# Block bounds by VectorE and one small product, in an attention and soft-MoE kernel

## The chip, the cores and the metric

The kernel runs on one core of one Trainium2 chip. The metric is the device time of one execution in microseconds (us). The times given for a kernel are those of repeated executions; one further execution was taken with the hardware profiler, and all rows of the trace come from that one.

Names used below: TensorE (PE in the profile; PEld its weight loads) does the matrix products and writes them into PSUM, 16 KB for each of 128 partitions in eight banks of 512 float32 values; VectorE (DVE) and ScalarE (ACT) read and write both PSUM and the on-chip SBUF; SyncE (SP) issues the DMAs.

## The reference, cut to what matters

```python
def _attn_ref(u, v, z):                  # u, v: (8, 2496, 256)   z: (8, 2496, 64)
    scores = (1.0 / S) * np.matmul(z, z.transpose(0, 2, 1))
    attn = np.maximum(scores, 0.0) ** 2
    return u * np.matmul(attn, v)

def _moe_ref(x, phi, w1, w2):            # x: (19968, 256)   phi: (256, 32)
    logits = x @ phi
    d = softmax of logits over all tokens (axis 0);  c = softmax over the 32 slots (axis 1)
    slot_input = (d.T @ x).reshape(8, 4, 256)
    slot_out[e] = np.maximum(slot_input[e] @ w1[e], 0.0) @ w2[e]    # for each of 8 experts
    return c @ slot_out.reshape(32, 256)
```

The inputs u, v and z are normal numbers times 0.1. Nothing of their size is assumed by the kernel: it scales blocks of z and v by powers of two before it splits them into a high and a low float16 part.

## The kernel before, in words

**Tiles.** A batch has 2496 rows, stored as five key blocks of 512 (the last padded). z of a block is a tile of 128 partitions by 512: the 64 features stand on the partitions, twice over. v of a block is two tiles of 128 by 512. Queries are worked through in chunks of 512 (chunk 4 of a batch is padded and has 448 columns). A chunk meets the five blocks in ten **halves** (256 keys each), so a batch has 50 halves, and the loop at the end of the kernel takes one half h per turn, called a step here. "Step 39" without a batch means the 40th step of a batch, the last half of chunk 3.

**A step.** `sums_halves` or `sums_whole` multiplies the half's attention (a high part ph and a low part pl) with v into the chunk's accumulator, a PSUM tile `acc` of two banks; the pool `acc_ps` holds two of them. In the same step `prepare` makes a half that comes two or three steps later: scores on TensorE (`sc`), Relu and Square on ScalarE (`r`), a cast to ph on ScalarE or VectorE, and pl by VectorE. Since z z^T is symmetric, half of the attention is transposed by VectorE (`y`), stored to DRAM (`turned`) and loaded again instead of being computed. When a chunk ends, `finish_chunk` multiplies its accumulator by u and by a factor (`out_by`) into `xg`. From `xg` the soft-MoE part is worked off in small pieces, one per step from the list `work`: logits, exponentials, transposes, sums of slots (`lg` in the trace).

**Order.** All engines keep the program order (class `InOrder`). Work that is to follow a prepared half is put on the list `behind`, which `prepare` runs at its end. `landing[h]` holds what joins `behind` in step h.

**Bounds and factors.** For each block of z in a batch b >= 1, `load_z` issues the load; two steps later `measure` lets ScalarE square the block (`squares`, tile sq), and again two or more steps later TensorE adds the squares over the features with a matrix of ones (`norms`, tile n in the trace, a PSUM tile of tag "ms") and VectorE takes the largest over each half block into `tops`. When five blocks are done, `factors` turns the largest sums into powers of two: `norm2` and, as its inverse root, `z_by`. v is handled by `load_v` (squares with a row sum into `energy`), `largest` in step 38 and `scale_v` in step 41: the latter spreads v's largest value over the partitions with two small products (mx in the trace, also of tag "ms"), VectorE reduces them into `few`, and `v_by` and `out_by` follow. The tag "ms" has one buffer (line 92), shared by n, mx and lg. `measure` keeps n and lg at least two steps apart.

**Opening.** For the first batch the same is written out ahead of the loop: squares and norms of the five blocks go to the tiles `n_first`, `n_second` and `idle`; the first halves are scored from raw float32 z (`zraw`, tile cw) scaled in place by `raise_z`; `keep_busy` issues matmuls whose result isn't used.

Of the kernel before, what the change touches and what calls it, by code (L numbers as in the profile page):

```python
# [8 lines left out]
F32 = mybir.dt.float32  # L9
# [9 lines left out]
P = 128  # L19
# [6 lines left out]
QC = 512  # L26
# [35 lines left out]
def bits(ap):  # L62
    return ap.bitcast(I32)
# [14 lines left out]
def attn_soft_moe_kernel(ctx, tc, uT, v, zz, phi, ww, outT):  # L78
# [29 lines left out]
    def pair(name, n):  # L108
# [3 lines left out]
        pair(name, n)  # L112
        for name, n in (("tops", 2 * NP), ("norm2", NP), ("z_by", NP), ("energy", 2 * NP), ("v_by", 2 * NP), ("out_by", NP), ("few", 4))
    )
# [9 lines left out]
    def load_z(b, j):  # L124


        if b == 0:
            raw = cw[:, 19 + 4 * j : 23 + 4 * j].rearrange("p g n -> p (g n)")
        else:
            raw = raws.tile([P, 512], F32, tag="raw", name=f"zr_{b}_{j}", bufs=NRAW)  # L130
        sp.dma_start(raw, zz[b, :, j * 512 : (j + 1) * 512])
        zraw[b, j] = raw
        by = z_by[b % 2][:, j : j + 1]
        square = []

        def squares():
            sq = raws.tile([P, 512], BF16, tag="sq", name=f"sq_{b}_{j}", bufs=2)
            act.activation(sq, raw, AF.Square, bias=nudge)
            square.append(sq)

        def norms(ps=None):
            if ps is None:
                ps = ms_ps.tile([P, 2, 512], F32, tag="ms", name=f"n2_{b}_{j}")[:, :, 0:256]
            for h, rows in enumerate(HALF):
                pe.matmul(
                    ps[:, h], ones[rows, 0:P], square[0][rows, 256 * h : 256 * h + 256],
                    start=True, stop=True,
                )
            dve.tensor_reduce(tops[b % 2][:, 2 * j : 2 * j + 2], ps, axis=AX.X, op=ALU.max)

        def split():
            t = zt[b, j]
            if b == 0:
                act.copy(t[:, 0], raw)
                dve.tensor_sub(t[:, 1], raw, t[:, 0])
            else:
                act.activation(t[:, 0], raw, AF.Identity, scale=by)
                dve.scalar_tensor_tensor(
                    t[:, 1], raw, by, t[:, 0], op0=ALU.mult, op1=ALU.subtract
                )  # L160

        return squares, norms, split
# [44 lines left out]

    def scale_v(b):


        w = few[b % 2]
        ps = ms_ps.tile([P, 2, 512], F32, tag="ms", name=f"mx_{b}")
        for h, rows in enumerate(HALF):
            pe.matmul(
                ps[:, h, 0:64], w[rows, 0:1].to_broadcast([64, P]), ident[rows, rows],
                start=True, stop=True,
            )
        dve.tensor_reduce(w[:, 2:4], ps[:, :, 0:64], axis=AX.X, op=ALU.max)
        dve.scalar_tensor_tensor(w[:, 1:2], w[:, 2:3], 2.0**-120, w[:, 3:4], op0=ALU.max, op1=ALU.max)
# [13 lines left out]
    def open_loads():  # L233
        for p in range(NP):
            *two, z_splits[p] = load_z(0, p)
            first_z.append(two)
        order = [i for p in range(NP) for i in ((2 * p + 1, 2 * p) if p == NQ - 1 else (2 * p, 2 * p + 1))]
# [344 lines left out]

    late, adding, bursts = [], [], []

# [20 lines left out]
    def groups(q):  # L605
# [17 lines left out]
        def logits():  # L623
# [4 lines left out]
            for c in range(2):  # L628
                for t in range(4):
                    for h, rows in enumerate(HALF):  # L630
# [3 lines left out]
                        )  # L634
            bursts.append(q)
            if late:
# [225 lines left out]
    for b in range(1, B):  # L862
# [12 lines left out]
    unmeasured, squared, used = [], [], [-9, 0]  # L875

    def measure(h, scoring):


        n = h % (2 * NP * NQ)  # L880
        if squared and squared[0][0] <= h - 2 and used[0] <= h - 2 and (scoring or n >= 26):
            behind.append(squared.pop(0)[1])
            used[0] = h
            used[1] += 1
            if used[1] % NP == 0:
                behind.append(lambda: factors(used[1] // NP))
        if unmeasured and unmeasured[0][0] <= h and len(squared) < 2:
            _, squares, norms = unmeasured.pop(0)
            behind.append(squares)
            squared.append((h, norms))  # L890

    def transfers(h):
# [14 lines left out]
        for f, b, i, at in splits.get(h + 2, ()):  # L907
            if (b, 0) not in vt_:
                take_blocks(b)
            if f is load_z:  # L910
                *two, split = f(b, i)
                unmeasured.append((h + 2, *two))
                landing.setdefault(at, []).append(split)
                continue
            for step, g in zip(at, f(b, i), strict=True):
# [38 lines left out]
    keep_busy(6)  # L954
    places = [ms_ps.tile([P, 2, 512], F32, tag="ms", name="n2_first")]
    places.append(acc_ps.tile([P, 2, QC], F32, tag="acc", name="n2_second"))
    places = [t[:, :, 256 * i : 256 * i + 256] for t in places for i in range(2)] + [idle[:, :, 0:256]]

    def raise_z(p):
# [5 lines left out]

    for p in range(NP):
        first_z[p][0]()
    first_z[0][1](places[0])
    factors(0, slice(0, 1))
    raise_z(0)  # L970
    for p in range(1, NP):
        keep_busy(1)
        first_z[p][1](places[p])
    factors(0, slice(1, NP))
    raise_z(1)
    for p in range(4):
        measure_v((2, 2, 1, 1)[p])
        prepare(p)
        if p < 3:
            raise_z(p + 2)  # L980
    keep_busy(8)
    measure_v(4)
    largest(0)
    scale_v(0)
    split_first_v()
    acc = None
    for h, x in enumerate(halves):
        if x.begins:
            acc = acc_ps.tile([P, 2, QC], F32, tag="acc", name=f"acc_{x.ch[3]}")
        last = len(halves) - h  # L990
        transfers(h)
        weights(last)
        if work and (x.at > 1 or last <= 20):
            n = len(bursts)
            work.pop(0)()
            if len(bursts) > n:
                used[0] = h
# [328 lines left out]
```

## Time and profile before

| | us |
|---|---|
| median of 3 runs | 1378.52 (1377.18 to 1385.05) |
| profiled execution | 1376.17 |
| its span, first to last instruction | 1374.0 |
| mean granted TensorE clock | 0.977 |

How to read it: the span lies 2.2 us under the time of the same execution, and that time 2.35 us under the median. A page of the profile gives busy time of each engine; the view of the waits lists how long an engine stood idle and whose end released it; the timeline lists instructions in order of time with their start, their length and, in brackets, the idle time before them and its releaser. In the trace all instructions have one line number (L74, the helper that keeps the order), so they are told apart by the names of their tiles, written "out<-in".

### The profile page before, as it was taken

Reading aid. Unit: us, or ns where it says so; the run is one execution under the profiler, and the core shown is the slowest. Engines: PE = TensorE matmul, PEld = TensorE weight load, DVE = VectorE, ACT = ScalarE, POOL = GpSimd, SP = SyncE. Lnnn points to the kernel's source line nnn. Section 1 sums busy time; section 2 is a strip of 40 time slices with the busy share of each in tenths; the row PEclk is TensorE's granted clock in tenths of the full one; section 3 lists DMA queues with packets and bytes.
Section 4 is the critical chain, followed back from the end, with each engine's and each line's share of the span. In section 5 each row is a group of like instructions: output and inputs, shape, how many; then the busy total and the mean of one; then the engine's idle time right before and its main releaser. Section 6 shows DMA issues by size and latency. Waiting matters only on the chain.

```text
span 1374.0 us, 27763 instructions
## 1 busy us (share of the span) xinstructions
PE 1275.1 (93%) x11029; PEld 618.3 (45%) x11029; DVE 1102.6 (80%) x1553; ACT 960.5 (70%) x1260; POOL 3.7 (0%) x22
## 2 busy tenths in 40 slices
PE   6998999899999999899999999989999999989984
PEld 2343445344544444344544444444454444434852
DVE  5687789688997799777998799877897799867663
ACT  6776778476876678567886678667786678754453
POOL 0000000000000000000000000000000000000000
PEclk9999999999999999999999999999999999999995
DMA  4566827777486856868287766868376776979959
GB/s 141 145 207 188 265 86 205 244 231 240 102 252 213 266 161 168 278 223 273 73 224 242 258 191 159 268 215 257 94 216 227 257 240 172 264 224 295 339 214 384
DMA packets 136401, 298.87 MB, mean 218 GB/s; under 512 B 17872, under 2 KB 38864, under 8 KB 124240
## 3 DMA queue, kind: packets, MB, share of 16 engines
q1 hardware_dynamic: 136272, 297.11, 69.4%
q8 instruction: 86, 1.41, 0.4%
q14 instruction: 43, 0.35, 0.1%
HBM read 162.04 MB, written 113.77 MB: 201 GB/s over the span
## 4 chain that ended last, share of the span: by engine, by line
PE 46%; ACT 17%; DVE 13%; DMA 11%; SPq 7%; issue 5%; DVEq 0%; ACTq 0%; POOLq 0%
PE acc L74 35%; ACT r L74 9%; SPq L74 7%; PE sc L74 5%; DMA turned<-y 5%; ACT ph L74 4%; DVE pl L74 4%; DVE y L74 4%; PE lg L74 2%; DMA vr<-in_v 2%; PE pf L74 1%; ACT vq L74 1%; DMA w_own<-in_w 1%; DVE ph L74 1%; DMA zr<-in_zz 1%
## 5 line engine op out<-in xcount | busy, mean ns | idle before, releaser
L74 PE MATMUL acc<-ph,v 64*128 64x512 f16 (+5 forms) x5036 | 934.9, 370 | 4.2 <-ACT v L74 1.8
L74 PEld LDWEIGHTS <-v 64*128 64x128 f16 (+1 forms) x7554 | 475.4, 95 | 525.8 <-issue 44.0
L74 PE MATMUL acc<-pl,v 64*128 64x512 f16 (+5 forms) x2518 | 604.1, 369 | 2.7 <-DVE pl L74 2.1
L74 DVE TENSOR_TENSOR pl<-r,ph 128x1024 f16<-128x1024 f32 (+1 forms) x410 | 466.5, 1146 | 146.6 <-ACT ph L74 133.7
L74 ACT CAST ph<-r 128x1024 f16<-128x1024 f32 (+1 forms) x286 | 287.5, 1017 | 87.6 <-DMA r<-turned 49.9
L74 ACT ACTIVATE r<-sc 128x1024 f32<-128x1024 f32 (+1 forms) x242 | 229.0, 946 | 140.6 <-PE sc L74 138.7
L74 ACT ACTIVATE r<-r 128x1024 f32<-128x1024 f32 (+1 forms) x242 | 238.5, 986 | 6.9
L74 DVE STREAM_TRANSPOSE y<-r 128x1024 f32<-128x1024 f32 x160 | 197.9, 1237 | 0.0
L74 PE MATMUL sc<-z,z 64*128 64x512 f16 x912 | 124.7, 377 | 7.8 <-ACT r L74 7.5
L74 PEld LDWEIGHTS <-z 64*128 64x128 f16 x1380 | 71.8, 94 | 86.0 <-issue 19.2
L74 DVE CAST ph<-r 128x1024 f16<-128x1024 f32 (+1 forms) x124 | 73.9, 596 | 21.9 <-ACT r L74 21.5
L74 ACT ACTIVATE vq<-vr 128x512 bf16<-128x512 f32 x80 | 49.8, 623 | 50.3 <-DMA vr<-in_v 49.8
L74 ACT ACTIVATE v<-vr,v_by 128x512 f16<-128x512 f32 x80 | 56.9, 715 | 11.8 <-DVE v_by L74 11.8
L74 DVE SCALAR_TENSOR_TENSOR xg<-acc,out_by,ut 128x1024 f32<-128x1024 f32 (+7 forms) x57 | 51.8, 931 | 13.3 <-PE acc L74 13.2
L74 DVE SCALAR_TENSOR_TENSOR v<-vr,v_by,v 128x512 f16<-128x512 f32 x80 | 57.8, 724 | 0.7 <-ACT v L74 0.7
L74 PE MATMUL sc<-z 64*128 64x512 f16 (+1 forms) x468 | 50.9, 321 | 2.9 <-ACT r L74 2.9
L74 PE MATMUL lg<-xg,phi_sb 64*32 64x256 f32 x608 | 25.5, 443 | 29.0 <-DVE tops L74 16.9
L74 DVE STREAM_TRANSPOSE y<-xg 128x512 f32<-128x512 f32 x72 | 49.4, 686 | 0.0
L74 ACT ACTIVATE sq<-zr,nudge 128x512 bf16<-128x512 f32 x35 | 25.0, 714 | 24.8 <-DMA zr<-in_zz 24.8
L74 DVE COPY ot<-pf 128x1024 f32<-128x1024 f32 (+1 forms) x20 | 24.0, 1198 | 20.6 <-PE pf L74 16.5
L74 ACT COPY ot<-pf 128x1024 f32<-128x1024 f32 (+1 forms) x20 | 19.8, 991 | 24.3 <-PE pf L74 18.1
L74 DVE TENSOR_TENSOR pl<-rd,ph 128x512 f16<-128x512 f32 x36 | 24.0, 668 | 11.3 <-ACT ph L74 11.1
(184 smaller groups left out, 579.7 us busy)
## 6 DMA issues: line engine op xcount, KB each, us to landing
turned<-y SPq DMA_DIRECT2D x320, 256.0 KB, 4.8
r<-turned SPq DMA_DIRECT2D x76, 1024.0 KB, 6.0
xt<-y SPq DMA_DIRECT2D x288, 72.0 KB, 2.9
vr<-in_v SPq DMA_DIRECT2D x80, 256.0 KB, 5.6
outT<-ot SPq DMA_DIRECT2D x18, 1024.0 KB, 7.4
ut<-in_uT SPq DMA_DIRECT2D x31, 512.0 KB, 5.6
lent<-yd SPq DMA_DIRECT2D x144, 64.0 KB, 2.8
rd<-lent SPq DMA_DIRECT2D x36, 256.0 KB, 4.0
```

Source lines behind the costliest of these rows:

```text
L74: return lambda *a, **k: self.tc.keep_in_program_order(f(*a, **k))
```

## The change

The bound of a z block is now the sum over the features of the largest square of each feature. VectorE takes the largest square of each of the 128 partitions in one instruction (`bound`), in place of ScalarE's squares, the product with ones and VectorE's reduction. When the five blocks are done, one product with a 128x128 matrix of ones adds the 128 values of each block (`add_bounds`), and `factors` reads the result. `add_bounds` runs in step 25 of a batch, `factors` in step 26; the product is written into the accumulator of the next chunk (chunk 3), which `next_acc` allocates for it ahead of time. `largest` moves from step 38 to 37 and `scale_v` from 41 to 39; its two products go into columns 448 to 511 of chunk 4's accumulator. `measure` and its guards are gone. In the opening the five bounds stand in VectorE's program order with their factors, all products go to `idle`, all of v's squares are taken after half 1 is prepared, and halves 2 and 3 are prepared after `scale_v`, half 2 ahead of the first split of v and half 3 behind it.

```diff
-        (("tops", 2 * NP), ("norm2", NP), ... , ("few", 4))
+        (("tops", NP), ("norm2", NP), ... , ("few", 4))
...
-        def squares():
-            sq = raws.tile([P, 512], BF16, tag="sq", name=f"sq_{b}_{j}", bufs=2)
-            act.activation(sq, raw, AF.Square, bias=nudge)
-            square.append(sq)
-
-        def norms(ps=None):
-            if ps is None:
-                ps = ms_ps.tile([P, 2, 512], F32, tag="ms", name=f"n2_{b}_{j}")[:, :, 0:256]
-            for h, rows in enumerate(HALF):
-                pe.matmul(
-                    ps[:, h], ones[rows, 0:P], square[0][rows, 256 * h : 256 * h + 256],
-                    start=True, stop=True,
-                )
-            dve.tensor_reduce(tops[b % 2][:, 2 * j : 2 * j + 2], ps, axis=AX.X, op=ALU.max)
+        def bound():
+            sq = raws.tile([P, 512], BF16, tag="sq", name=f"sq_{b}_{j}", bufs=1)
+            dve.tensor_tensor_reduce(
+                sq, raw, raw, 1.0, 2.0**-80, op0=ALU.mult, op1=ALU.max,
+                accum_out=tops[b % 2][:, j : j + 1],
+            )
...
-    def factors(b, js=slice(0, NP)):
+    def add_bounds(b, ps, js):
+        pe.matmul(
+            ps[:, 0, js], nc.const_aps.tensor(1.0, [P, P], F32), tops[b % 2][:, js], start=True, stop=True
+        )
+
+    def factors(b, ps, js):
...
-        t = tops[b % 2].rearrange("p (j h) -> p h j", h=2)[:, :, js]
-        dve.tensor_max(n2, t[:, 0], t[:, 1])
-        dve.tensor_scalar(bits(n2), bits(n2), EVEN, None, op0=ALU.bitwise_and)
+        dve.tensor_scalar(bits(n2), bits(ps[:, 0, js]), EVEN, None, op0=ALU.bitwise_and)
...
-    def scale_v(b):
+    def scale_v(b, ps):
...
-        ps = ms_ps.tile([P, 2, 512], F32, tag="ms", name=f"mx_{b}")
+        ps = ps[:, :, 2 * PAD :]
         for h, rows in enumerate(HALF):
             pe.matmul(
-                ps[:, h, 0:64], w[rows, 0:1].to_broadcast([64, P]), ident[rows, rows],
+                ps[:, h], w[rows, 0:1].to_broadcast([64, P]), ident[rows, rows],
                 start=True, stop=True,
             )
-        dve.tensor_reduce(w[:, 2:4], ps[:, :, 0:64], axis=AX.X, op=ALU.max)
+        dve.tensor_reduce(w[:, 2:4], ps, axis=AX.X, op=ALU.max)
...
         for i, (j, at) in enumerate(zip(order, z_at)):
-            splits.setdefault(base + 11 + 2 * i, []).append((load_z, b, j, base + at))
+            splits.setdefault(base + 11 + 2 * i, []).append((load_z, b, j, [base + 14 + 2 * i, base + at]))
...
-        later[base + 38] = lambda b=b: largest(b)
-        later[base + 41] = lambda b=b: scale_v(b)
+        later[base + 37] = lambda b=b: largest(b)
+        later[base + 39] = lambda b=b: scale_v(b, next_acc())
+        later[base + 25] = lambda b=b: add_bounds(b, next_acc(), slice(0, NP))
+        later[base + 26] = lambda b=b: factors(b, accs[-1], slice(0, NP))
...
-    def measure(h, scoring):
...
+    def next_acc():
+
+        accs.append(acc_ps.tile([P, 2, QC], F32, tag="acc", name=f"acc_{len(accs)}"))
+        return accs[-1]
...
-    for p in range(NP):
-        first_z[p][0]()
-    first_z[0][1](places[0])
-    factors(0, slice(0, 1))
-    raise_z(0)
-    for p in range(1, NP):
-        keep_busy(1)
-        first_z[p][1](places[p])
-    factors(0, slice(1, NP))
-    raise_z(1)
-    for p in range(4):
-        measure_v((2, 2, 1, 1)[p])
-        prepare(p)
-        if p < 3:
-            raise_z(p + 2)
+    for js in (slice(0, 1), slice(1, 2), slice(2, NP)):
+        for p in range(*js.indices(NP)):
+            first_z[p]()
+        add_bounds(0, idle, js)
+        factors(0, idle, js)
+        if js.start < 2:
+            raise_z(js.start)
+            keep_busy(2)
+    prepare(0)
+    measure_v(2)
+    prepare(1)
+    measure_v(8)
     keep_busy(8)
-    measure_v(4)
+    for p in range(2, NP):
+        raise_z(p)
     largest(0)
-    scale_v(0)
+    scale_v(0, idle)
+    prepare(2)
     split_first_v()
+    prepare(3)
     acc = None
     for h, x in enumerate(halves):
         if x.begins:
-            acc = acc_ps.tile([P, 2, QC], F32, tag="acc", name=f"acc_{x.ch[3]}")
+            chunk = h // (2 * NP)
+            acc = accs[chunk] if chunk < len(accs) else next_acc()
...
-        measure(h, ahead and not halves[ahead[0]].turned)
```

More of the change, by code (lines that the diff above doesn't have):

```diff
@@ L112, in attn_soft_moe_kernel @@
         pair(name, n)
-        for name, n in (("tops", 2 * NP), ("norm2", NP), ("z_by", NP), ("energy", 2 * NP), ("v_by", 2 * NP), ("out_by", NP), ("few", 4))
+        for name, n in (("tops", NP), ("norm2", NP), ("z_by", NP), ("energy", 2 * NP), ("v_by", 2 * NP), ("out_by", NP), ("few", 4))
     )
@@ L133, in load_z @@
         by = z_by[b % 2][:, j : j + 1]
-        square = []
-        def squares():
-            sq = raws.tile([P, 512], BF16, tag="sq", name=f"sq_{b}_{j}", bufs=2)
-            act.activation(sq, raw, AF.Square, bias=nudge)
-            square.append(sq)
-        def norms(ps=None):
-            if ps is None:
-                ps = ms_ps.tile([P, 2, 512], F32, tag="ms", name=f"n2_{b}_{j}")[:, :, 0:256]
-            for h, rows in enumerate(HALF):
-                pe.matmul(
-                    ps[:, h], ones[rows, 0:P], square[0][rows, 256 * h : 256 * h + 256],
-                    start=True, stop=True,
-                )
-            dve.tensor_reduce(tops[b % 2][:, 2 * j : 2 * j + 2], ps, axis=AX.X, op=ALU.max)
+        def bound():
[4 more added lines that the diff above has]
+            )
         def split():
@@ L160, in split @@
                 )
-        return squares, norms, split
-    def factors(b, js=slice(0, NP)):
+        return bound, split
+    def add_bounds(b, ps, js):
[3 more added lines that the diff above has]
+    def factors(b, ps, js):
         n2, by = (t[b % 2][:, js] for t in (norm2, z_by))
-        t = tops[b % 2].rearrange("p (j h) -> p h j", h=2)[:, :, js]
-        dve.tensor_max(n2, t[:, 0], t[:, 1])
-        dve.tensor_scalar(bits(n2), bits(n2), EVEN, None, op0=ALU.bitwise_and)
+        dve.tensor_scalar(bits(n2), bits(ps[:, 0, js]), EVEN, None, op0=ALU.bitwise_and)
         dve.tensor_scalar(
@@ L234, in open_loads @@
         for p in range(NP):
-            *two, z_splits[p] = load_z(0, p)
-            first_z.append(two)
+            bound, z_splits[p] = load_z(0, p)
+            first_z.append(bound)
         order = [i for p in range(NP) for i in ((2 * p + 1, 2 * p) if p == NQ - 1 else (2 * p, 2 * p + 1))]
@@ L581, in finish_chunk @@
             s += w
-    late, adding, bursts = [], [], []
+    late, adding = [], []
     xt_last = []
@@ L634, in logits @@
                         )
-            bursts.append(q)
             if late:
@@ L871, in attn_soft_moe_kernel @@
             )
-        later[base + 38] = lambda b=b: largest(b)
-        later[base + 41] = lambda b=b: scale_v(b)
+        later[base + 37] = lambda b=b: largest(b)
+        later[base + 39] = lambda b=b: scale_v(b, next_acc())
+        later[base + 25] = lambda b=b: add_bounds(b, next_acc(), slice(0, NP))
+        later[base + 26] = lambda b=b: factors(b, accs[-1], slice(0, NP))
     landing, fetched = {}, set()
-    unmeasured, squared, used = [], [], [-9, 0]
-    def measure(h, scoring):
[L880 to L890, printed above, removed]
+    accs = []
+    def next_acc():
+        accs.append(acc_ps.tile([P, 2, QC], F32, tag="acc", name=f"acc_{len(accs)}"))
+        return accs[-1]
     def transfers(h):
@@ L909, in transfers @@
                 take_blocks(b)
[L910 to L914, printed above, removed]
             for step, g in zip(at, f(b, i), strict=True):
@@ L954, in attn_soft_moe_kernel @@
     keep_busy(6)
-    places = [ms_ps.tile([P, 2, 512], F32, tag="ms", name="n2_first")]
-    places.append(acc_ps.tile([P, 2, QC], F32, tag="acc", name="n2_second"))
-    places = [t[:, :, 256 * i : 256 * i + 256] for t in places for i in range(2)] + [idle[:, :, 0:256]]
     def raise_z(p):
@@ L993, in attn_soft_moe_kernel @@
         if work and (x.at > 1 or last <= 20):
-            n = len(bursts)
             work.pop(0)()
-            if len(bursts) > n:
-                used[0] = h
         behind.extend(landing.pop(h, ()))
         ahead = [k for k in range(h + 2 + (h > CATCH), h + 3 + (h >= CATCH)) if k < len(halves) and k >= 4]
-        measure(h, ahead and not halves[ahead[0]].turned)
         split_first_v()
```

## The prediction

> **What bounds the kernel now.** I read the page first, then the waits of TensorE, then the timeline around each of those waits, and only then the other engines.
>
> ```profile
> span 1374.0 us, 27763 instructions
> PE 1275.1 (93%) x11029; PEld 618.3 (45%) x11029; DVE 1102.6 (80%) x1553; ACT 960.5 (70%) x1260; POOL 3.7 (0%) x22
> ```
>
> TensorE is busy for 93% of the span, so the question is what its 99 us of idle time consist of. The view of the waits, for TensorE alone, answers it:
>
> ```profile
> PE lg L74 <- DVE tops L74: 16.9, 4, 4.7
> ...
> PE lg L74 <- DVE few L74: 12.1, 4, 3.3
> PE n L74 <- DVE tops L74: 8.8, 9, 1.8
> ...
> PE mx L74 <- DVE few L74: 3.6, 2, 3.2
> PE n L74 <- DVE slot_acc L74: 3.0, 3, 1.0
> ```
>
> The first column is the total, then the number of waits, then the longest. All five rows have one cause: the tag "ms" has a single buffer, and logits (lg), norms (n) and the product for v's factor (mx) take turns in it. TensorE may not write the next until VectorE, which runs some us behind, has read the last. 3.2 us of the mx row are in the opening, so 16.9 + 12.1 + 8.8 + 3.0 + 0.4 = **41.2 us** of idle TensorE in the steady part hang on the buffer that this change leaves to the logits alone.
>
> Some of these waits cost more than their length:
>
> ```profile
> 268.75 1.96 PE L74 MATMUL lg<-xg,phi_sb 64*32 64x256 f32 x32 [4.72 <-DVE tops L74]
> 270.46 1.90 PE L74 MATMUL lg<-xt 64*32 64x256 f32 x32
> ...
> 517.41 1.09 PE L74 MATMUL lg<-xg,phi_sb 64*32 64x256 f32 x32
> 518.30 1.07 PE L74 MATMUL lg<-xt 64*32 64x256 f32 x32
> ...
> 268.70:270.00 1.30, 1.25 (x24) 0.67 (x32) 0.00 (x0) 0.00 (x0) 0.00 (x0) 0.52 0.43 105
> ...
> 173.32 1.96 PE L74 MATMUL lg<-xg,phi_sb 64*32 64x256 f32 x32 [3.30 <-DVE few L74]
> ...
> 962.86 1.10 PE L74 MATMUL lg<-xg,phi_sb 64*32 64x256 f32 x32 [3.17 <-DVE few L74]
> ```
>
> The same burst of 64 matmuls takes 3.61 us after a wait of 4.72 us (268.75 to 272.36) and 1.96 us without one (517.41 to 519.37). The row of the windows view shows why: the granted clock (third number from the end) is 0.52. A wait of 3.30 us still has it (1.96 for 32 matmuls), one of 3.17 us has not (1.10). So a wait over about 3.2 us costs 1.65 us on top. Five of the eight logits waits are that long (the four for tops and the first for few); I count 1.5 each, 7.6 us.
>
> **The change, part by part.** *What goes.* The 41.2 us of waits and 7.6 us of half clock. Then the 35 pairs of norm matmuls:
>
> ```profile
> 103.29 0.27 PE L74 MATMUL n<-sq,const-bfloat16-1.0 64*128 64x256 bf16 x2
> 103.40 0.59 PE L74 MATMUL acc<-ph,v 64*128 64x512 f16 x4
> ...
> L74 ACT ACTIVATE sq<-zr,nudge 128x512 bf16<-128x512 f32 x35 | 25.0, 714 | 24.8 <-DMA zr<-in_zz 24.8
> ...
> L74 DVE TENSOR_REDUCE tops<-n 128x2 f32<-128x512 f32 x35 | 22.8, 652 | 0.0
> ...
> L74 DVE SCALAR_TENSOR_TENSOR z<-zr,z_by,z 128x512 f16<-128x512 f32 x35 | 26.1, 745 | 0.0
> ...
> 97.83 0.59 PE L74 MATMUL acc<-ph,v 128*128 128x512 f16 x2 [0.64 <-ACT ph L74]
> ```
>
> The next matmul starts 0.11 us after the pair: 35 x 0.11 = 3.9 us. ScalarE loses 25.0 us of squares and the 24.8 us in which it stood at the head of its queue waiting for z. Both are off TensorE's path except in the first batch, where full sums wait for ScalarE's high part (97.83, and two like it); I take 1 us for it (bounds 0 and 2). Removed in all: 41.2 + 7.6 + 3.9 + 1 = **53.7 us**.
>
> *What VectorE gets.* One multiply-and-max of 128x512 per block in place of a reduction of 128x512. The trace has no such instruction of this size; the nearest are the reduction and the z row above, 652 and 745 ns. At 0.7 us, 35 of them add 1.7 us to VectorE, and the 7 maxima of two halves that go give about that back. It stands five steps behind its load instead of two, so it waits for no DMA, and no DMA issue is moved on SyncE. I cost it at nothing; at the two ends, 652 and 745 ns, VectorE gains or loses some 3 us in the whole run, spread over steps in which it is idle 20% of the time.
>
> *What TensorE gets.* Seven products of 128x128 by 5 columns. Nearest is the mx product (quoted below, 0.44 us for two); I take 0.3 each, 2 us (bounds 0.5 and 4). They are written five steps before chunk 3 begins and read one step later, so nothing waits for that read.
>
> *What moves: the product for v's factor.* It goes from step 41 of a batch to step 39, out of "ms" into columns 448 to 511 of chunk 4's accumulator. Chunk 4 sums only into columns 0 to 447, so no byte is shared, but the opening shows what a write beside a read does here:
>
> ```profile
> 4.62 0.69 DVE L74 TENSOR_REDUCE tops<-n_first 128x2 f32<-128x512 f32 x1 [3.76 <-PE n_first L74]
> ...
> 5.37 0.39 PE L74 MATMUL n_first<-sq,const-bfloat16-1.0 64*128 64x256 bf16 x2 [0.36 <-DVE tops L74]
> ```
>
> VectorE read columns 0 to 255 of both banks of n_first until 5.31; the matmuls at 5.37 wrote columns 256 to 511 of the same tile, and waited for that read. The order is kept by the bank, not by the column. So chunk 4's first sums must wait until VectorE has reduced mx, and VectorE has other work first. Here is that place in the first batch, TensorE and VectorE:
>
> ```profile
> 164.35 0.54 PE L74 MATMUL acc<-ph,v 128*128 128x448 f16 x2
> 167.20 0.44 PE L74 MATMUL mx<-ident,few 64*128 64x64 f32 x4 [0.42 <-DVE few L74]
> ...
> 167.06 1.27 DVE L74 SCALAR_TENSOR_TENSOR xg<-acc,out_by,ut 128x1024 f32<-128x1024 f32 x1
> 168.25 1.22 DVE L74 TENSOR_TENSOR pl<-r,ph 128x1024 f16<-128x1024 f32 x1
> 169.39 0.74 DVE L74 SCALAR_TENSOR_TENSOR z<-zr,z_by,z 128x512 f16<-128x512 f32 x1
> 170.05 2.35 DVE L74 TENSOR_TENSOR pl<-r,ph 128x1024 f16<-128x1024 f32 x2
> ...
> 1113.56 0.54 PE L74 MATMUL acc<-ph,v 128*128 128x448 f16 x2
> 1118.80 2.35 DVE L74 TENSOR_TENSOR pl<-r,ph 128x1024 f16<-128x1024 f32 x2
> ...
> L74 DVE TENSOR_REDUCE few<-mx 128x2 f32<-128x128 f32 x8 | 2.3, 284 | 0.9 <-PE mx L74 0.9
> ```
>
> Chunk 4 (448 columns) begins at 164.35. Step 39 queues on VectorE: chunk 3's output product (xg), the low part of half 42 (pl), the low part of a z block (z), and then the reduction of mx, where the next pl stands now, at 170.05. With 0.04 us between instructions, 0.28 for it and 0.06 to TensorE, chunk 4 would begin at 170.43, or 6.1 us late. Read in the same way the last batch gives 1118.80 + 0.38 - 1113.56 = 5.6, and the five between give 5.1, 5.7, 5.1, 5.6 and 5.5: 38.7 in all. The mx matmuls (0.4 us, moved, not new) run inside it, which leaves **36 us** of new idle time, 4.7 to 5.7 at a time. Each is longer than 3.3, so each brings the half clock: 7 x 1.65 = **11.5 us**. What is queued behind the wait is all of chunk 4; VectorE and ScalarE work on, and run ahead of TensorE afterwards, with no gain.
>
> The Trainium skill speaks against this place too: PSUM — Partial Sum Buffer, section on bank collisions, says to guard PSUM by bank and quadrant and not by address, because two engines at disjoint columns of a bank still collide. By that rule the wait is needed and stays; the row at 5.37 agrees.
>
> *The opening.* Now TensorE's first full sums are at 29.98, and ScalarE is the chain:
>
> ```profile
> 8.74 1.92 PE L74 MATMUL sc<-cw 64*128 64x512 f32 x4
> ...
> 17.27 1.02 ACT L74 ACTIVATE r<-sc 128x1024 f32<-128x1024 f32 x1 [0.48 <-PE sc L74]
> 20.37 0.62 ACT L74 ACTIVATE vq<-vr 128x512 bf16<-128x512 f32 x1
> ...
> 25.24 0.63 ACT L74 ACTIVATE vq<-vr 128x512 bf16<-128x512 f32 x1
> ...
> 28.42 2.56 ACT L74 ACTIVATE v<-vr,v_by 128x512 f16<-128x512 f32 x4 [2.45 <-DVE v_by L74]
> 29.98 0.61 PE L74 MATMUL acc<-ph,v 64*128 64x512 f16 x2 [0.18 <-DVE v L74]
> ```
>
> Afterwards five bounds run one behind another on VectorE with two factors and two scalings between them, so the first scores start near 10.7 instead of 8.74. ScalarE then has only two halves (2.1 us each) and ten squares of v (0.75 each) before v's factor, which ends near 24.5 instead of 26.0. But half 2 is then prepared ahead of v's first split: its scores wait for mx, and its three ScalarE passes take 3.1 us (17.27 to 20.37). v's first block is split near 31.1, VectorE does half 2's low part first, and full sums begin near 33: **+2.8 us** at step 2 (bounds +1 and +4.5).
>
> *The sum.* -53.7 + 36 + 11.5 + 2 + 2.8 = -1.4 us. The profiled execution took 1376.17 us, 2.2 more than its span, which gives 1374.8. The runs of before have their median at 1378.52, 2.35 above the profiled one, so I forecast **1377 us** for a median: no change that can be told, since a measurement of this kernel separates about 0.5% (6.9 us).
>
> **The rivals.** *A shorter wait.* Were VectorE not behind at that place, the wait would be the four instructions alone: 1.19 + 1.14 + 0.66 + 0.38 = 3.4 us, 3.0 without mx, and the clock would stay. That is 7 x 3.0 = 21 in place of 47.5: 1350 us. For it: VectorE loses three reductions between steps 25 and 28. Against: it is filled anew by steps 36 to 39, 2.7 us behind at 167.06 (164.35). Chance 0.20, 1349 to 1369.
>
> *The clock stays.* If an idle time of about 5 us doesn't bring the half clock, some or all of the 11.5 us go: 1366 to 1371. Against it: after the waits of 3.30 and 4.72 us it came. Chance 0.05. The rule behind this rival is in the Trainium skill, TensorE: Matmul & The Clock Gate, section "What's actually happening": the clock drops after an idle window of about 3.4 us, and the windows run freely, so that a wait of 5 us can fall across two of them. By that rule half of the seven waits would escape; the rows above don't bear it out.
>
> *No wait.* If the columns are told apart, chunk 4 starts at once and 47.5 us of my sum go: 1330 us, chance 0.07, since the row at 5.37 says otherwise.
>
> *Slower.* In the four batches with logits waits TensorE gains some 6 to 9 us before step 40 (a wait of 4 to 5 us, its half clock, and most of the waits of n), and v's loads do not get faster with it:
>
> ```profile
> 462.15 0.63 ACT L74 ACTIVATE vq<-vr 128x512 bf16<-128x512 f32 x1 [5.85 <-DMA vr<-in_v]
> 471.28 0.82 PE L74 MATMUL sc<-z,z 64*128 64x512 f16 x6 [1.63 <-ACT r L74]
> ...
> 302.90 0.63 ACT L74 ACTIVATE vq<-vr 128x512 bf16<-128x512 f32 x1 [2.75 <-DMA vr<-in_v]
> ```
>
> In the batch at 462 ScalarE waits 5.85 us for v and scores wait for it; at 302.90 it waits 2.75 and nothing follows. From about 4 us on it decides. Some 2.5 us in each of four batches would be 1387 us: 0.18.
>
> **How the numbers follow.** Forecast 0.50 (its own range 1369 to 1385), shorter wait 0.20, clock stays 0.05, no wait 0.07, slower 0.18. Faster by over 0.5% (below 1371.6): 0.05 of the forecast, 0.19 of the shorter wait, 0.04 and 0.07 of the next two, 0.35. Slower (above 1385.4): 0.04 of the forecast and 0.14 of the last, 0.18. The rest, 0.47, is no change. The range takes in the slower case and the upper half of the shorter wait, 1356 to 1389, and leaves out no wait and the shortest ones.
>
> **What would show it.** Right: no wait of lg for tops or few; instead a wait of acc for few, seven times, 4.7 to 5.7 us, before the first 448-column matmul, with a granted clock near 0.5 after it; first full sums near 33 us. Wrong: that wait missing or near 3 us with the clock at 1; lg waiting for something else; more of sc waiting for ScalarE near step 34.

## The result, and the profile after

| | us |
|---|---|
| before, median of 6 runs | 1379.92 (1377.18 to 1385.05) |
| after, median of 6 runs | 1391.05 (1389.26 to 1393.29) |
| ratio | 1.0076, 95% interval 1.0052 to 1.0100 |
| profiled execution after | 1392.14 (span 1390.4, mean granted clock 0.962) |

The changed kernel is slower, by 11 us between the medians and by 16.0 us between the two profiled executions (1376.17 and 1392.14). The forecast was 1377, with a range up to 1389.

The head of the page:

```profile
span 1390.4 us, 27647 instructions
PE 1283.8 (92%) x10969; PEld 617.5 (44%) x10969; DVE 1101.2 (79%) x1587; ACT 936.1 (67%) x1220; POOL 3.7 (0%) x22
```

TensorE has 60 matmuls fewer than before and is busy 8.7 us longer: some of the same work ran at a lower clock. The view of TensorE's waits (total, number, longest) shows which waits replaced the old ones:

```profile
PE acc L74 <- DVE few L74: 38.3, 14, 4.4
PE sc L74 <- ACT r L74: 14.7, 28, 1.7
...
PE idle L74 <- DVE few L74: 6.8, 1, 6.8
PE lg L74 <- DMA xt<-y: 6.6, 6, 1.8
PE lg L74 <- DMA lent<-yd: 5.2, 1, 5.2
```

No logits wait for tops or few any more, and there are no norms left to wait. In their place stand 14 waits of the accumulator for few. (The row of idle is the opening, the one of lent the last batch.) The view of the groups of instructions (busy time and mean, then idle time ahead of them and its releaser) splits those 14 in two:

```profile
L74 PE MATMUL acc<-ph,v 64*128 64x512 f16 (+5 forms) x5036 | 944.5, 372 | 34.1 <-DVE few L74 30.1
...
L74 PE MATMUL acc<-ident,few 64*128 64x64 f32 x28 | 3.1, 296 | 8.2 <-DVE few L74 8.2
```

30.1 us are chunk 4's first sums, seven times; 8.2 us are the product for v's factor itself, which waits for its own operand. Both can be seen in the timeline of batch 3's end, on TensorE:

```profile
642.37 0.44 PE L74 MATMUL acc<-ident,few 64*128 64x64 f32 x4 [2.58 <-DVE few L74]
647.18 0.91 PE L74 MATMUL acc<-ph,v 128*128 128x448 f16 x2 [4.37 <-DVE few L74]
647.88 0.58 PE L74 MATMUL acc<-pl,v 128*128 128x448 f16 x1
648.25 0.95 PE L74 MATMUL acc<-ph,v 128*128 128x448 f16 x2
...
652.34 0.54 PE L74 MATMUL acc<-ph,v 128*128 128x448 f16 x2
```

The pair of matmuls that takes 0.54 us at 652.34 takes 0.95 at 648.25, behind the wait of 4.37 us. VectorE at the same place, from the wait of the product to the one of the sums:

```profile
639.22 0.69 DVE L74 CAST ph<-r 128x1024 f16<-128x1024 f32 x1 [2.26 <-ACT r L74]
...
642.15 0.16 DVE L74 TENSOR_REDUCE few<-v_by 128x1 f32<-128x10 f32 x1
...
643.77 1.36 DVE L74 SCALAR_TENSOR_TENSOR xg<-acc,out_by,ut 128x384 f32<-128x384 f32 x2
645.05 1.22 DVE L74 TENSOR_TENSOR pl<-r,ph 128x1024 f16<-128x1024 f32 x1
646.18 0.74 DVE L74 SCALAR_TENSOR_TENSOR z<-zr,z_by,z 128x512 f16<-128x512 f32 x1
646.85 0.28 DVE L74 TENSOR_REDUCE few<-acc 128x2 f32<-128x128 f32 x1
```

Lower half: the queue that the prediction named, xg, pl, z and then the reduction, 3.36 us from 643.77 to 647.13, and chunk 4 starts 0.05 us later. (Ahead of xg, in the rows left out, stand one more low part and a transpose.) Upper half: few is late (642.15) because the high part at 639.22 waited 2.26 us for ScalarE's r. And r was late because of this row of ScalarE's timeline:

```profile
636.46 0.63 ACT L74 ACTIVATE vq<-vr 128x512 bf16<-128x512 f32 x1 [2.53 <-DMA vr<-in_v]
```

ScalarE stood 2.53 us at the head of its queue, in front of v's last block, with the scores' Relu and Square behind it.

For the whole span I lined up the first full-sum matmul of each step in the two timelines and took the difference in a step's length, summed over the seven batches that have a next one (us, after minus before; the last batch is taken up to its last full sum):

| place | predicted | after |
|---|---|---|
| opening, to the second step | +2.8 | +3.6 |
| steps 0 to 29 | -37.7 | -35.5 |
| steps 30 to 38 | 0 | +8.6 |
| step 39, to chunk 4's first sums | +38.7 | +42.5 |
| steps 40 and 41 | -5.2 | -5.0 |
| last batch | 0 | +1.8 |
| all | -1.4 | +16.1 |

The predicted column is the prediction's sum, put where its terms lie: in steps 0 to 29 the waits for tops and of n, four half clocks, the norm matmuls, the first batch's 1 us and add_bounds; in step 39 the 38.7 us of delay; in steps 40 and 41 the waits for few with their half clock and the product that left (16.7 us), against 11.5 us of new half clock.

### The profile page after: what moved, and what is told of

It reads as the page before. It is cut to its first block, busy times and chain, and to the rows that moved or that the text cites. A ratio compares the mean times of both kernels' runs of the same rounds, so it can differ in the third digit from the quotient of the medians.

```text
span 1390.4 us, 27647 instructions
## 1 busy us (share of the span) xinstructions
PE 1283.8 (92%) x10969; PEld 617.5 (44%) x10969; DVE 1101.2 (79%) x1587; ACT 936.1 (67%) x1220; POOL 3.7 (0%) x22
## 4 chain that ended last, share of the span: by engine, by line
PE 52%; DMA 14%; ACT 12%; DVE 9%; SPq 6%; issue 5%; DVEq 0%; ACTq 0%; POOLq 0%
PE acc L74 40%; PE sc L74 7%; SPq L74 6%; ACT r L74 6%; DMA r<-turned 4%; DMA vr<-in_v 4%; ACT ph L74 3%; DVE pl L74 3%; DVE y L74 2%; PE lg L74 2%; DMA turned<-y 2%; PE pf L74 1%; DMA w_own<-in_w 1%; ACT vq L74 1%; DMA xt<-y 1%
## 5 line engine op out<-in xcount | busy, mean ns | idle before, releaser
L74 PE MATMUL acc<-ph,v 64*128 64x512 f16 (+5 forms) x5036 | 944.5, 372 | 34.1 <-DVE few L74 30.1
L74 PE MATMUL lg<-xt 64*32 64x256 f32 x576 | 24.8, 402 | 12.1 <-DMA xt<-y 6.6
L74 ACT CAST ph<-rd 128x512 f16<-128x512 f32 x36 | 21.8, 605 | 11.6 <-DMA rd<-lent 11.6
```

What stands on the lines that cost most here:

```text
L74: return lambda *a, **k: self.tc.keep_in_program_order(f(*a, **k))
```

## Experiments

Each run has the kernel before beside it on the same chip; the ratio is to that, with its 95% interval. The table puts all of them, profiled executions alone, against the kernel before, by the places of the table above (us; the columns are opening, steps 0 to 29, 30 to 38, 39, 40 to 49, last batch, all). It is worked out in the same way, and the text below speaks of its columns.

| run | opening | 0-29 | 30-38 | 39 | 40-49 | last | all |
|---|---|---|---|---|---|---|---|
| the changed kernel | 3.6 | -35.5 | 8.6 | 42.5 | -5.0 | 1.8 | 16.1 |
| e1_mx_own_tile | 3.1 | -33.2 | 9.9 | 9.3 | -17.9 | -2.3 | -31.1 |
| e2_mx_first | 3.4 | -36.1 | 7.2 | 20.4 | -11.3 | -1.8 | -18.1 |
| e3_warm | 3.4 | -34.7 | 8.2 | 41.5 | -18.0 | 0.1 | 0.5 |
| e4_old_opening | 2.1 | -36.3 | 10.9 | 39.7 | -2.7 | -1.9 | 11.7 |
| e5_own_tile_old_opening | 1.7 | -35.6 | 8.0 | 10.3 | -16.2 | -0.7 | -32.5 |
| e6_v_steps_as_before | 2.6 | -33.2 | 9.0 | 0.0 | 6.1 | 1.1 | -14.4 |
| e7_scores_first | -0.3 | -36.6 | 9.6 | 8.7 | -17.9 | -0.8 | -37.3 |
| e8_v_squares_later | 1.7 | -35.9 | 0.0 | 16.9 | -16.2 | 3.1 | -30.5 |
| e9_product_step_40 | -0.9 | -33.8 | 9.8 | 9.9 | -14.2 | 1.7 | -27.6 |
| e10_largest_step_36 | -0.2 | -36.4 | 7.9 | 3.2 | -16.0 | -1.5 | -43.0 |

Two or three us in one field are the spread from one execution to the next: the last batch is the same code in most rows and lies between -2.3 and 3.1. The runs stand on three chips (e1 to e4, e5 to e8, e9 and e10), on which the kernel before has medians of 1381.23, 1378.65 and 1383.14 us, so a few us between runs of two groups say little.

### The product in its own tile: e1_mx_own_tile

```diff
-        ps = ps[:, :, 2 * PAD :]
+        ps = ms_ps.tile([P, 2, 512], F32, tag="ms", name=f"mx_{b}")[:, :, 0:64] if ps is None else ps[:, :, 2 * PAD :]
...
-        later[base + 39] = lambda b=b: scale_v(b, next_acc())
+        later[base + 39] = lambda b=b: scale_v(b, None)
```

> The changed kernel with v's factor's two products back in a tile of tag ms, still in step 39. Theory A (chunk 4 waits only because the reduction of mx reads its banks): the seven waits of acc for few (4.25 to 4.37 us each, 30 in all) and the half clock behind them (about 1.5 each) go, some 40 us of the changed kernel's 1392 (profiled), so about 1350; the wait of mx for few stays. Theory B (TensorE has outrun VectorE, ScalarE and v's loads, and would stand still a few steps later anyway): less than half of that comes, 1375 or more, with new waits of acc for pl or sc for r in chunk 4.

Measured: 1347.36 us, 0.9763 (0.9718 to 0.9807), profiled 1345.03. TensorE's timeline at the same place of batch 3:

```profile
619.59 0.44 PE L74 MATMUL mx<-ident,few 64*128 64x64 f32 x4 [1.32 <-DVE few L74]
619.96 0.55 PE L74 MATMUL acc<-ph,v 128*128 128x448 f16 x2
```

Chunk 4 follows the product at once and at full speed. Nothing but the place of the product was changed, and 47.1 us went between the profiled executions (1392.14 to 1345.03). The forecast had put 36 + 11.5 = 47.5 us on this wait and its half clock. By the medians, each against the kernel before beside it, it is 43 us. Of the 47.1, 33.2 us are delay (step 39) and 12.9 lie behind it (steps 40 to 49), against 36 and 11.5 in the forecast; the other 1.0 is the net of columns that the edit doesn't touch, so that the sums agree to 0.4 us is luck. The wait on the bank is more than the whole loss, and without it the change gains 2.4%. Two things this run leaves open. It changes the tile together with the bank, and chunk 4's accumulator is one tile of two whole banks, so no run tells whether the order hangs on the bank or on the tile. And the wait is one for VectorE's semaphore, set by the program; no run lets both engines into one bank at once.

### The reduction ahead of VectorE's queue: e2_mx_first

```diff
-        later[base + 39] = lambda b=b: scale_v(b, next_acc())
+        at_end[base + 39] = lambda b=b: scale_v(b, next_acc())
...
             sums_whole(h, acc)
+        if h in at_end:
+            at_end[h]()
         if x.ends:
             finish_chunk(x.b, x.ch, acc)
```

> The changed kernel with v's factor made directly behind step 39's sums, ahead of the end of chunk 3 on VectorE, still in chunk 4's accumulator. If the price of the shared bank is VectorE's queue ahead of the reduction (xg, pl, z: 3.1 us), the seven waits of acc for few shrink from 4.3 to about 1 us and the clock stays: 7 x (3.2 + 1.5) = 33 us less, about 1359. If the price lies elsewhere (mx itself, or its arrival), it stays near 1391.

Measured: 1361.45 us, 0.9856 (0.9824 to 0.9889). The bank is still shared; only what stands ahead of the reduction on VectorE has changed. From TensorE's waits, from VectorE's timeline between few and the reduction, and from TensorE's timeline in two batches:

```profile
PE acc L74 <- DVE few L74: 16.2, 14, 2.1
```

```profile
470.74 1.22 DVE L74 TENSOR_TENSOR pl<-r,ph 128x1024 f16<-128x1024 f32 x1
471.88 0.44 DVE L74 STREAM_TRANSPOSE y<-E 128x256 f32<-128x256 f32 x1
472.24 0.25 DVE L74 TENSOR_REDUCE few<-acc 128x2 f32<-128x128 f32 x1
```

```profile
470.85 0.44 PE L74 MATMUL acc<-ident,few 64*128 64x64 f32 x4 [1.22 <-DVE few L74]
472.54 0.54 PE L74 MATMUL acc<-ph,v 128*128 128x448 f16 x2 [1.26 <-DVE few L74]
...
1096.15 0.90 PE L74 MATMUL acc<-ph,v 128*128 128x448 f16 x2 [1.26 <-DVE few L74]
...
1097.22 0.95 PE L74 MATMUL acc<-ph,v 128*128 128x448 f16 x2
```

The waits for few fall from 38.3 to 16.2 us. What the shared bank costs is the reader's queue: with xg, pl and z behind the reduction 32.5 of the 47.1 us come back (profiled 1359.64), 28.4 of them in steps 39 to 49. The last two rows show a half clock behind a wait of only 1.26 us, where the one at 472.54 has none; this comes back below.

### TensorE kept busy in the wait: e3_warm

```diff
-        later[base + 39] = lambda b=b: scale_v(b, next_acc())
+        later[base + 39] = lambda b=b: (scale_v(b, next_acc()), stay_warm())
...
+    def stay_warm():
+        ps = ms_ps.tile([P, 2, 512], F32, tag="ms", name="warm")
+        for _ in range(13):
+            for h, rows in enumerate(HALF):
+                pe.matmul(ps[:, h], ones[rows, 0:P], ones[rows], start=True, stop=True)
```

> The changed kernel with 26 more matmuls whose result isn't used, behind mx and ahead of chunk 4's sums, in a tile of tag ms (2.8 us of TensorE inside the wait). The waits end at the same time, so the idle part is what changes. If the half clock after the wait is brought by the idle time, chunk 4 starts at full clock and 7 x 1.0 to 1.65 us go: about 1380 to 1384, granted clock 1.0 after the wait. If the slow sums after the wait have another cause, 1391 or a little more.

Measured: 1379.58 us, 0.9985 (0.9961 to 1.0008). The same wait in batch 0, first with the 26 matmuls (timeline, then the view of stretches, whose third number from the end is the granted clock), then in the changed kernel:

```profile
161.55 3.01 PE L74 MATMUL warm<-const-bfloat16-1.0 64*128 64x512 bf16 x26
165.97 0.54 PE L74 MATMUL acc<-ph,v 128*128 128x448 f16 x2 [1.41 <-DVE few L74]
```

```profile
166.00:167.40 1.40, 1.40 (x8) 0.75 (x8) 1.33 (x5) 0.00 (x0) 0.00 (x0) 1.00 1.07 367
```

```profile
166.10:167.40 1.30, 1.30 (x4) 0.53 (x4) 1.23 (x5) 0.00 (x0) 0.00 (x0) 0.50 0.97 380
```

The sums start no earlier (step 39 costs 41.5 us, against 42.5), but at clock 1.00 instead of 0.50, and steps 40 and 41 give -18.0 us instead of -5.0. That is 13.0 us of half clock in seven waits, 1.86 each, where the prediction had 1.65 each.

### The opening in its old order: e4_old_opening

```diff
-    prepare(0)
-    measure_v(2)
-    prepare(1)
-    measure_v(8)
+    for p in range(4):
+        measure_v((2, 2, 1, 1)[p])
+        prepare(p)
+        if p < 3:
+            raise_z(p + 2)
     keep_busy(8)
-    for p in range(2, NP):
-        raise_z(p)
+    measure_v(4)
     largest(0)
     scale_v(0, idle)
-    prepare(2)
     split_first_v()
-    prepare(3)
```

> The changed kernel with the order of before in the opening behind the bounds (halves 0 to 3 prepared between v's squares, v's factor after them). By the trace the new order puts step 2 at 40.6 instead of 37.0 us. If that comes from half 2 being prepared between v's factor and v's first split: 2 to 4 us less, about 1388, first full sums near 30 us. If it comes from the five bounds standing in VectorE's order ahead of the first scores: no change, full sums near 32.

Measured: 1389.73 us, 1.0061 (1.0039 to 1.0084). Medians don't tell it from the changed kernel. The first full sums in the timeline of the changed kernel, and then the first scores and full sums here:

```profile
32.95 0.61 PE L74 MATMUL acc<-ph,v 64*128 64x512 f16 x2 [0.69 <-DVE v L74]
```

```profile
11.03 2.08 PE L74 MATMUL sc<-cw 64*128 64x512 f32 x4
...
32.43 0.61 PE L74 MATMUL acc<-ph,v 64*128 64x512 f16 x2 [0.18 <-DVE v L74]
```

The second step of the loop starts 1.5 us earlier, still 2.1 us later than before the change, and the first scores still start at 11.03 instead of 8.74. So of the 3.6 us in the opening 1.5 hang on the order of the halves, the rest on something ahead of the first scores. The forecast for this run, full sums near 30, was too hopeful.

### Both: e5_own_tile_old_opening

The two edits above, e1's and e4's, together.

> The product for v's factor in its own tile as in e1_mx_own_tile, and the opening in the order of the kernel before. If the two parts are independent, the opening gives what e4_old_opening gave against the changed kernel (the second step of the loop starts 1.5 us earlier in its trace), so about 1.5 us under e1_mx_own_tile: span near 1341.7, ratio to before near 0.975. If the order of the opening shifts later steps against v's loads, it can come out 2 to 3 us to either side.

Measured: 1343.62 us, 0.9738 (0.9708 to 0.9767); profiled 1343.50, 1.5 under e1's. The opening costs 1.7 us here and 3.1 in e1. The next runs start from this one.

### v's factor in its old steps: e6_v_steps_as_before

```diff
-        later[base + 37] = lambda b=b: largest(b)
-        later[base + 39] = lambda b=b: scale_v(b, None)
+        later[base + 38] = lambda b=b: largest(b)
+        later[base + 41] = lambda b=b: scale_v(b, None)
```

> As e5_own_tile_old_opening, but the largest of v in step 38 and the product for v's factor in step 41, as in the kernel before. Theory that the earlier step pays: the waits of the logits for few come back (12.1 us in the kernel before, one of four with the half clock, 1.65), the waits of the product itself go (5.5), so about 8 us over e5, near 1350. Rival, that the removal of the norms alone empties VectorE enough: the waits of the logits for few are under 2 us each or absent, and the time is within 3 us of e5 or under it.

Measured: 1360.49 us, 0.9855 (0.9819 to 0.9891), 17 us over e5. TensorE's waits:

```profile
PE lg L74 <- DVE few L74: 13.4, 4, 3.4
```

The logits of step 41 wait for few four times, as before, 3.35 us each. The rival, that VectorE without the norms' reductions would be in time, falls. Where the move acts, steps 39 to 49, it is worth 12.0 us (0.0 + 6.1 here, 10.3 - 16.2 in e5), more than the 8 expected, since the half clock follows all four of these waits here and only one in the kernel before. The other 6 us between the two profiled executions are spread over the columns that the edit doesn't touch.

### The scores ahead of the last three bounds: e7_scores_first

```diff
-    for js in (slice(0, 1), slice(1, 2), slice(2, NP)):
-        for p in range(*js.indices(NP)):
-            first_z[p]()
+    for js in (slice(0, 1), slice(1, 2)):
+        first_z[js.start]()
         add_bounds(0, idle, js)
         factors(0, idle, js)
...
+    for p in range(2, NP):
+        first_z[p]()
     for p in range(4):
         measure_v((2, 2, 1, 1)[p])
         prepare(p)
+        if p == 0:
+            add_bounds(0, idle, slice(2, NP))
+            factors(0, idle, slice(2, NP))
```

> As e5, but the first half's scores are issued ahead of the product for the last three bounds. If the three bounds in front of the first scores are what makes the opening late (scores at 11.0 instead of 8.7 us), full sums begin near 30.3 instead of 32.4 us in the trace: 2 us, too little to tell from the medians. If the factors of blocks 2 to 4 then come too late for half 2's scores, full sums stay over 31.5 us.

Measured: 1339.72 us, 0.9726 (0.9687 to 0.9766). TensorE's timeline in the opening, e5 and then e7:

```profile
10.08 0.59 PE L74 MATMUL idle<-tops,const-float32-1.0 128*128 128x3 f32 x2 [2.10 <-DVE tops L74]
10.59 2.08 PE L74 MATMUL sc<-cw 64*128 64x512 f32 x4
...
31.99 0.61 PE L74 MATMUL acc<-ph,v 64*128 64x512 f16 x2 [0.18 <-DVE v L74]
```

```profile
8.33 1.94 PE L74 MATMUL sc<-cw 64*128 64x512 f32 x4
10.50 0.58 PE L74 MATMUL idle<-tops,const-float32-1.0 128*128 128x3 f32 x2 [0.23 <-DVE tops L74]
...
29.57 0.61 PE L74 MATMUL acc<-ph,v 64*128 64x512 f16 x2 [0.18 <-DVE v L74]
```

The first scores need only block 0's factor, but stood behind a product that waited 2.10 us for three bounds which they don't use. With the two exchanged, full sums start 2.4 us earlier, and the opening costs -0.3 us instead of e5's 1.7.

### v's squares a step later: e8_v_squares_later

```diff
-                (load_v, b, i, [base + 27 + i, base + at, base + at])
+                (load_v, b, i, [base + 28 + i, base + at, base + at])
...
-        later[base + 37] = lambda b=b: largest(b)
-        later[base + 39] = lambda b=b: scale_v(b, None)
+        later[base + 38] = lambda b=b: largest(b)
+        later[base + 40] = lambda b=b: scale_v(b, None)
```

> As e5, but ScalarE squares each block of v one step later (three steps behind its load instead of two), the largest in step 38 and the product for v's factor in step 40. Theory that ScalarE standing in front of v's loads is what holds scores and few back: its waits for vr fall from about 62.7 us to under 45, scores waiting for r from 16.1 to under 11, the product's waits for few from 5.5 to under 3; 4 to 8 us under e5 unless the logits of step 41 then wait for few (0 to 1.5 us each). Rival, that the DMA engines are simply full: the waits for vr move to another place and scores wait as long as before, time within 3 us of e5.

Measured: 1341.05 us, 0.9718 (0.9681 to 0.9756), not to be told from e5. Waits of ScalarE in e5, then of TensorE and ScalarE in e8:

```profile
ACT vq L74 <- DMA vr<-in_v: 67.3, 22, 6.3
```

```profile
PE mx L74 <- DVE few L74: 13.2, 7, 2.2
...
PE sc L74 <- ACT r L74: 11.7, 24, 1.3
```

```profile
ACT vq L74 <- DMA vr<-in_v: 53.4, 19, 6.3
```

Half of the expectation came: ScalarE waits 14 us less in front of v's loads, scores wait 11.7 us instead of 16.4, and steps 30 to 38, which cost 7 to 11 us in every other row, cost nothing here. That nothing is a net of two: scores also stopped waiting in batches 2, 4 and 6, where they did before the change, while the loss of step 31 (3.5 us, logits waiting for x's DMA) is still there. But the largest is a step later too, and the product now waits 13.2 us for few instead of 6.5: step 39 costs 16.9 us instead of 10.3. The gain came back as another wait. By its time this run meets the rival's condition (within 3 us of e5), by its waits for r it doesn't; whether the DMA engines are simply full isn't settled.

### The product in step 40: e9_product_step_40

```diff
-        later[base + 39] = lambda b=b: scale_v(b, None)
+        later[base + 40] = lambda b=b: scale_v(b, None)
```

> As e7_scores_first, but the product for v's factor in step 40, own tile. In e7 the product's wait for few is 5.0 us in seven and its reduction ends 0.26 us ahead of the logits of step 41 (619.67 and 619.93). Theory that the price is the reader's queue: one step later the reduction stands behind one more low part of two halves (2.35 us) and a z block (0.74), so the logits of step 41 wait for few, about 3 us in four batches, and the 5 us of the product's wait go: 4 to 10 us over e7, near 1346. Rival, that only the product's wait counts: 5 us under e7, near 1335.

Measured: 1349.09 us, 0.9757 (0.9708 to 0.9807), profiled 1348.51 against e7's 1338.76 (on another chip). The time is near the first theory's, but not for its reason:

```profile
PE mx L74 <- DVE few L74: 6.2, 7, 2.1
...
PE lg L74 <- DVE few L74: 3.3, 4, 0.9
```

The logits wait for few as named, but 0.8 us each instead of 3, and the product's own waits did not go. On TensorE the edit moves nothing: the product still stands right behind chunk 3's sums and right ahead of chunk 4's, and it is its reduction on VectorE that comes later. 3.7 us of the difference to e7 lie in steps 40 and 41, where these waits are, 2.5 in the last batch and 2.8 in steps 0 to 29, which the edit doesn't touch. The intervals of e7 and e9 overlap, so neither theory is settled by the time; by the rows both are wrong in part.

### The largest in step 36: e10_largest_step_36

```diff
-        later[base + 37] = lambda b=b: largest(b)
+        later[base + 36] = lambda b=b: largest(b)
```

> As e7_scores_first, but the largest of v in step 36, in the step of v's last square. Theory that the product waits for few only because few stands late in VectorE's order: its 5.0 us of waits go, time 3 to 5 us under e7. Rival, that few is late because v's last square on ScalarE is late (it waits for v's load): VectorE then waits for ScalarE at that place, its next low parts come later, and the product waits as long or sums wait instead; within 3 us of e7 or over it.

Measured: 1334.28 us, **0.9659 (0.9623 to 0.9694)**, the fastest version of all, though its interval just meets e7's. The product at the end of batch 3, and its group, which had 8.2 us of idle time in the changed kernel:

```profile
612.27 0.44 PE L74 MATMUL mx<-ident,few 64*128 64x64 f32 x4
```

```profile
L74 PE MATMUL mx<-ident,few 64*128 64x64 f32 x28 | 3.1, 296 | 0.0
```

few is taken ahead of the late high part instead of behind it, and no product waits. Step 39 costs 3.2 us, about what the product takes seven times (0.44). Profiled it is 1333.04, 5.7 under e7 (on another chip), where 3 to 5 were expected of the waits alone. The logits of step 41 now wait for few twice, 1.6 us in all.

## Why the prediction was wrong, point by point

**Right: what is removed.** The waits of logits, norms and product on the buffer of "ms" went. Steps 0 to 29 gained 35.5 us of 37.7. Of the missing 2.2 us about 1 is add_bounds, 0.42 us in each batch where it can be read alone, instead of 0.3; and the logits of step 21, which no longer wait for tops, wait for the DMA of x instead in batches 3 and 5 (1.38 and 1.24 us).

**Right: the bank wait and its price.** "So chunk 4's first sums must wait until VectorE has reduced mx" was put at 47.5 us with the half clock; e1 measured 47.1 by moving the product out of the bank. The steps of the working hold as well: the queue xg, pl, z, reduction is in the trace in that order, e2 shows that it is that queue which costs, and e3 that the half clock is 13.0 us where 11.5 was said. The rival of a shorter wait (the four instructions alone, 1350 us) fell: VectorE was behind as forecast. That the clock might stay, or the columns be told apart, fell too: all seven waits are there, and behind all seven the clock is half.

**Wrong: the cost of bringing the product forward.** "The mx matmuls (0.4 us, moved, not new) run inside it" took for granted that few is ready by then. The product itself waits for few, 8.2 us in seven, 2.58 the longest. The delay at chunk 4's start was meant to be 38.7 us and was 42.5, since the two waits partly share the time. The cause is one that the prediction quoted for something else: ScalarE in front of v's loads (5.85 us at 462.15). I followed what is queued behind the moved step, but not what the step itself needs: few is now taken one step after v's last square instead of two, and used two steps later instead of three.

**Wrong: one rival was not a rival.** "Slower", TensorE getting ahead of v's loads so that scores wait for ScalarE, had 0.18 and 2.5 us in each of four batches. Steps 30 to 38 gave back 8.6 us, 0.9 to 2.5 in each of batches 1 to 5. TensorE's waits for r there grew by 2.0 us and those of logits for x's DMA by another 2.0, and behind one of these the clock is half (in batch 2 steps 31 and 32 are 4.0 us longer, 1.84 of it the wait). One of the waits for r, in batch 1, before and then after; its step is 0.62 us longer:

```profile
317.35 0.49 PE L74 MATMUL sc<-z 64*128 64x256 f16 x6
```

```profile
307.86 0.50 PE L74 MATMUL sc<-z 64*128 64x256 f16 x6 [0.45 <-ACT r L74]
```

So the mechanism is partly another than I named: x's loads, not only v's. e8 shows v's share, since scores wait less when ScalarE comes to v's loads later; how the rest divides stays open. Nor are the batches those that I named, the four whose logits had waited (0, 1, 3 and 5): batch 0, which gained 6.9 us in steps 0 to 29, gave nothing back, and batches 2 and 4, which gained 2.3 each, gave back 2.5 and 1.8. So the loss doesn't go with the gain, and that the gain brings it is not shown; that the total is near the 10 us which I had priced is luck. But it needs nothing of the forecast to be false, so it could come on top of it and belonged in the sum, where I had put steps 30 to 38 at nothing. 1377 with those 10 is 1387, with the 3.8 of the product 1391, and that this meets the median is luck again: between the profiled executions the forecast is off by 17.5 us (-1.4 against 16.1), of which these two steps measure 12.4 and the rest is the smaller misses here, while the profiled execution lies 1.1 us over its median after the change and lay 2.35 under it before. And the loss belonged in the range, which I made from cases that exclude each other, so that its top was the forecast plus one of them.

**Small misses.** The opening cost 3.6 us instead of 2.8. I had the scores' later start, but put it down to five bounds in a row; by e4 and e7 1.5 us hang on the order of the halves and 2.0 on one product in TensorE's order ahead of scores that don't need it. The last batch, which I put at nothing, lost 1.8 us. That is within what this column does from run to run.

**By its own signs.** Of those listed as right all came, but for a size: the wait of acc for few is 4.25 to 4.37 us where 4.7 to 5.7 was said, since the product's own wait had already taken part of it. Of those listed as wrong, two came as well: logits waiting for something else (x's DMA), and scores waiting for r in more batches near step 35.

## What to carry to other kernels

Let two small products share a PSUM tile, and with it its banks, only if the reader of the first has little queued ahead of it: the price of the sharing was not the 0.28 us reduction but VectorE's work in front of it (3.1 us of xg, pl and z in batch 3), plus a half clock, seven times. When a step is brought forward, follow its operands back as far as what waits behind it: here the product met a DMA's lateness two engines upstream, and moving the operand forward as well (e10) took away the last of the product's waits. A wait that is removed on the bounding engine can let it run into the next engine's limit. Here 33 to 37 us gained in steps 0 to 29 stand beside 7 to 11 lost in steps 30 to 38, in every version but e8; price such a loss in the sum, even where no row yet says which batch will have it.

## What the runs showed of the hardware that I had not expected

The length of a wait doesn't decide alone whether the clock drops. The prediction read a limit of about 3.2 us from two waits. In the changed kernel a wait of 1.84 us is enough (timeline, then three stretches around it):

```profile
453.35 2.17 PE L74 MATMUL lg<-xt 64*32 64x256 f32 x32 [1.84 <-DMA xt<-y]
```

```profile
451.50:453.30 1.80, 0.00 (x1) 0.00 (x0) 1.47 (x2) 0.82 (x1) 0.00 (x0) 1.00 0.97 244
453.35:454.65 1.30, 1.30 (x25) 0.92 (x32) 0.23 (x1) 0.00 (x0) 0.00 (x0) 0.73 0.96 372
454.65:456.00 1.35, 1.35 (x19) 0.28 (x3) 0.00 (x0) 0.00 (x0) 0.00 (x0) 0.50 0.89 312
```

The clock falls from 1.00 to 0.50 within the burst that follows, after work has begun again. In e2 two waits of 1.26 us, each 0.4 us of work behind a wait of 1.22, stand at 472.54 and 1096.15, and only the second drops the clock. Between 40 and 1290 us of the twelve traces every wait of TensorE from 3.28 us on was followed by a half clock, in it or within 1.3 us of its end; the one of 3.17 us in the kernel before was not.

What decides is where the wait falls. In all twelve traces the granted clock changes only at points that lie a whole number of 3.413 us apart (to within 0.003 us), and between 40 and 1290 us it stays half for one or two such stretches. Where TensorE was idle for more than 2.0 us of a stretch at full clock, the next one had the half clock; with less than 1.7 us none had; in between both occur. The wait of 1.84 us lies whole in one stretch (450.54 to 453.95). In e2 the two short waits at 1096.15 fall into one stretch with 2.4 us idle, those at 472.54 into two with 1.3 and 1.1; and the 3.17 us before the change fell into two with 2.0 and 1.2. The Trainium skill, TensorE: Matmul & The Clock Gate, section "What's actually happening", describes such a window, free-running, of about 3.4 us, after which the clock drops if it was idle. The traces agree with its length and with the free running, but a window that was idle for a little over half was enough here.

For a price this means: a wait of over 4 us has more than 2 us in one of the stretches that it touches, however it falls, and can be charged the half clock, 1.65 to 1.86 us here, as all seven waits of the changed kernel show. One of 1 to 4 us can be charged a part of it.
